# Filter taps carried through DRAM, part of q's feature map on ScalarE, and one transpose for the last 64 features of two chunks

## The chip, the core and the metric

The kernel runs on one core of a Trainium2 chip. The core has a matrix engine (TensorE, in the profile PE, with its weight loads listed apart as PEld), VectorE (DVE), ScalarE (ACT), GpSimd (POOL), and SyncE (SP), which here only issues DMAs. Each engine runs its own instructions in the order in which the program lists them, and waits where data from another engine is missing. The metric is the time of one execution on the device in microseconds (us); smaller is better.

## The reference

The result mixes two branches by a gate, for S = 2048 tokens of D = 448 features:

```python
g = sigmoid((x * gate_w).sum(-1, keepdims=True))
a = A(x, wqkv, wo)          # linear attention, 16 heads of 28 features
b = B(x, ...)               # long convolution along the tokens, plus x * D_skip
return g * a + (1 - g) * b

# A
phi = lambda t: where(t > 0, t + 1, exp(t)) + 1e-6
pq, pk = phi(q), phi(k)
kv = einsum("bhsd,bhse->bhde", pk, v);  z = einsum("bhsd->bhd", pk)
o = einsum("bhqd,bhde->bhqe", pq, kv) / (einsum("bhqd,bhd->bhq", pq, z) + 1e-6)
return o @ wo
```

B convolves every feature with a filter that is built from `log_A_real`, `A_imag`, `C_real`, `C_imag` and `log_dt`.

## The kernel before

The tokens are cut into 16 chunks of 128. Products in near-fp32 precision are made of fp32r pieces: a matrix is split into a rounded high part and the low remainder, and a product takes the high-high, low-high and high-low terms. So one projection of a chunk is 11 matmuls with 128 x 128 weights and about 448 moving columns. The schedule is written by hand: the order of the calls is the order on each engine.

**Start.** `first_d`, the other weights, x and the filter's parameters `abc` (four DMAs of 448 KB, lines 229-230) arrive by DMAs on SP. `load_x` brings in one chunk, `split_t` and `split_n` make its transposed and plain high and low parts (high on ACT, low on POOL).

**Filter.** `s4d_prepare` is a generator that `steps` advances between other work. It computes for each feature whether its filter is a constant over all lags, to the precision needed (`okc`), and the value of that constant (`p0`, 112 partitions x 4). Features that are not constant would need `general_conv`, which is behind a branch at the end and is not entered with these inputs. The generator's last part (lines 311-314) spreads `p0` over 128 partitions: four transposes on PE into the bank "v1", and a copy on ACT into `near`. `do_v(c)` multiplies a chunk by the triangular matrix `tri` (running sums along the tokens, two matmuls), `v_post(c)` multiplies the running sums by `near` on DVE, sends the last row by two small DMAs to `u`, and lets POOL add the product to `y` (`v_add`).

**Main loop** (line 476, c = 2 to 13). An iteration projects k of chunk c+1 (`project`, bank "k"), runs `k_feature`, `k_high`, `k_low` on it, projects q of chunk c (bank "q"), runs `q_post`, and accumulates `do_g(c)`, ten matmuls of pk's parts with x into four banks that stay open over all chunks. `VS` (line 35) lists which `do_v` go into which iteration. `q_post` uses `feature`: exp on ACT, then on DVE a clamp (`t = min(e, 1) + 1e-6`, line 350) and `max(q + 1 + 1e-6, t)` into `pq` (line 353). In iteration 5 come the four transposes (`steps(1)`, line 496), `v_post(0)`, `do_v(1)` and `v_post(1)`.

**Middle.** After chunk 15's k the sums are turned into `kv`, which is multiplied with `wo` to give the rows `mh`, `ml`.

**Attention loop** (line 814, c = 0 to 15). For each chunk `norm_a` (POOL) and `norm_b` (DVE) form the denominators, `norm_d` inverts them for two chunks at a time (DVE, then a copy on ACT, line 556), and `norm_c` divides pq by them into `pn`, a tile of 4 x 128 columns: three column blocks j = 0, 1, 2 of 112 + 16 features, and a block j = 3 that holds the last 64 features twice (POOL, line 573). `turn_pe` transposes the four blocks on PE into the PSUM tile "tr" (line 604), `turn_split` makes the high part `th` on ACT (line 611) and the low part `tl` on DVE (line 612). In block 3 the transposed features stand in partitions 0 to 63 and again in 64 to 127, since one half meets the high and the other the low part of the weights. `tail` (line 615) puts rows for the convolution's part of earlier chunks into the low part. `attend` multiplies with 11 matmuls (line 629), and `final_b` adds y and sends the chunk out. The loop runs `turn(c+1)` ahead of `attend(c)`.

## Time and profile before

| What | Value |
|---|---|
| Time, median of 3 runs | 173.89 us (173.82 to 174.45) |
| The profiled execution's own time | 174.06 us |
| Its span, first to last instruction | 172.2 us |
| Instructions | 2796 |
| Bytes moved by DMA | 18.60 MB, mean 108 GB/s |

The busy time in the stages, as the view by windows gives it:

| Stage | us from the start | PE | DVE | ACT | POOL |
|---|---|---|---|---|---|
| start, first chunks | 5.0 to 46.6 | 41.60 | 30.32 | 30.08 | 26.51 |
| rest of the main loop | 47 to 118 | 71.00 | 40.35 | 35.33 | 55.33 |
| middle | 118 to 127 | 9.00 | 8.06 | 5.81 | 7.69 |
| attention, chunks 0 to 11 | 127 to 158 | 31.00 | 28.28 | 17.49 | 26.42 |
| attention, the rest | 158 to 169 | 11.00 | 5.47 | 4.68 | 1.11 |

A row of the profile's timeline reads: start, length, engine, line of the kernel, operation, tile written <- tiles read, shape, count, and in brackets the idle time before it and what ended it. Matmuls overlap each other, so their pace is read from start to start and not from their length. A group row of the view by lines ends in busy time and the mean length of one in ns, then the idle time before.

### The profile page before, as it was taken

Reading aid. Unit: us, or ns where it says so; the run is one execution under the profiler, and the core shown is the slowest. Engines: PE = TensorE matmul, PEld = TensorE weight load, DVE = VectorE, ACT = ScalarE, POOL = GpSimd, SP = SyncE. Lnnn points to the kernel's source line nnn. Section 1 sums busy time; section 2 is a strip of 40 time slices with the busy share of each in tenths; the row PEclk is TensorE's granted clock in tenths of the full one; section 3 lists DMA queues with packets and bytes.
Section 4 is the critical chain, followed back from the end, with each engine's and each line's share of the span. In section 5 each row is a group of like instructions: output and inputs, shape, how many; then the busy total and the mean of one; then the engine's idle time right before and its main releaser. Section 6 shows DMA issues by size and latency. Waiting matters only on the chain. (4 is left out here: it accounts for less than half of the span.)

```text
span 172.2 us, 2796 instructions
## 1 busy us (share of the span) xinstructions
PE 167.8 (97%) x876; PEld 152.0 (88%) x876; DVE 113.9 (66%) x240; ACT 96.0 (56%) x221; POOL 120.0 (70%) x128
## 2 busy tenths in 40 slices
PE   6999999999999999999999999999999999999992
PEld 2788999999899999999999999999899999999992
DVE  0847737698975483846627346487898998987542
ACT  3688588894256262542727456356574564664541
POOL 6082667877529988696996999529968998892200
PEclk9999999999999999999999999999999999999999
DMA  5989975097003031230404200000031222122213
GB/s 173 415 297 294 268 209 166 0 368 303 4 0 114 11 123 34 95 123 1 122 15 131 106 1 1 0 0 2 7 67 54 107 89 76 62 99 107 108 59 108
DMA packets 7962, 18.60 MB, mean 108 GB/s; under 512 B 2045, under 2 KB 4810, under 8 KB 7818
## 3 DMA queue, kind: packets, MB, share of 16 engines
q1 hardware_dynamic: 7802, 18.30, 32.0%
q8 instruction: 7, 0.11, 0.3%
q10 hardware_dynamic: 144, 0.11, 0.2%
q14 instruction: 9, 0.07, 0.1%
HBM read 14.38 MB, written 3.67 MB: 105 GB/s over the span
## 5 line engine op out<-in xcount | busy, mean ns | idle before, releaser
L629 PE MATMUL a<-wk,th 128*128 128x448 f32 (+1 forms) x170 | 36.4, 360 | 0.0
L403 PE MATMUL g<-pkh,xn 128*128 128x448 f32 x112 | 35.6, 364 | 0.0
L629 PEld LDWEIGHTS a<-wk,th 128*128 128x128 f32 x170 | 29.5, 189 | 1.6
L334 PE MATMUL k<-wk,xt 128*128 128x448 f32 x132 | 29.3, 367 | 0.0
L334 PE MATMUL q<-wqh,xt 128*128 128x450 f32 x120 | 27.5, 366 | 0.0
L362 DVE SCALAR_TENSOR_TENSOR k<-k,e 128x448 f32<-128x448 f32 x12 | 7.6, 632 | 29.4 <-ACT e L361 29.4
L423 POOL TENSOR_TENSOR y<-y,t 128x448 f32<-128x448 f32 x16 | 18.7, 1168 | 11.5 <-DVE t L415 11.5
L334 PEld LDWEIGHTS k<-wk,xt 128*128 128x128 f32 x132 | 24.8, 189 | 2.2 <-DVE wk L236 0.3
L334 PEld LDWEIGHTS q<-wqh,xt 128*128 128x128 f32 x120 | 22.5, 188 | 1.7
L236 POOL TENSOR_TENSOR xn<-xr,xn 128x448 fp32r<-128x448 f32 x16 | 19.4, 1211 | 6.6 <-ACT xn L246 4.5
L403 PE MATMUL g<-pkl,xn 128*128 128x448 f32 x64 | 23.4, 366 | 0.0
L403 PEld LDWEIGHTS g<-pkh,xn 128*128 128x128 f32 x112 | 21.0, 188 | 2.2
L236 POOL TENSOR_TENSOR xt<-xr,xt 128x512 fp32r<-128x512 f32 x14 | 18.2, 1297 | 5.9 <-ACT xt L240 5.9
L360 ACT ACTIVATE e<-k 128x448 f32<-128x448 f32 x12 | 6.5, 544 | 26.9 <-PE k L334 26.9
L542 POOL TENSOR_TENSOR prod<-pq,zb 128x448 f32<-128x448 f32 x16 | 18.6, 1172 | 4.1 <-ACT zb L665 3.0
L252 POOL TENSOR_TENSOR y<-xr,rows 128x448 f32<-128x448 f32 x16 | 18.8, 1175 | 0.0
L567 POOL TENSOR_TENSOR pn<-pq,den 128x336 f32<-128x336 f32 x16 | 12.3, 771 | 5.9 <-ACT den L556 4.1
L634 DVE SCALAR_TENSOR_TENSOR ot<-y,og,a 128x448 f32<-128x448 f32 (+1 forms) x17 | 10.7, 629 | 5.1 <-PE a L629 5.1
L612 DVE TENSOR_TENSOR th<-tr,th 128x512 fp32r<-128x512 f32 x16 | 11.0, 691 | 2.7 <-ACT th L611 2.1
L403 PEld LDWEIGHTS g<-pkl,xn 128*128 128x128 f32 x64 | 11.2, 174 | 1.2 <-DVE pkl L372 0.2
L611 ACT CAST th<-tr 128x512 fp32r<-128x512 f32 x16 | 9.4, 588 | 4.6 <-PE tr L604 4.4
L334 PE MATMUL q<-wql,xt 128*128 128x450 f32 x45 | 11.6, 364 | 0.0
(150 smaller groups left out, 302.3 us busy)
## 6 DMA issues: line engine op xcount, KB each, us to landing
xr<-in SPq DMA_DIRECT2D x15, 512.0 KB, 6.2
out<-ot SPq DMA_DIRECT2D x15, 224.0 KB, 1.9
pq<-in SPq DMA_DIRECT2D x4, 448.0 KB
wvo<-in SPq DMA_DIRECT2D x1, 1792.0 KB
y<-in SPq DMA_DIRECT2D x2, 480.0 KB
y<-in SPq DMA_DIRECT2D x2, 450.0 KB
u<-t SPq DMA_DIRECT2D x30, 1.8 KB, 1.7
y<-in SPq DMA_DIRECT2D x1, 448.0 KB, 4.3
```

What stands on the lines that cost most here:

```text
L236: eng.tensor_tensor(out=o, in0=r, in1=h.bitcast(F32), op=ALU.subtract)
L252: POOL.tensor_tensor(out=y[:, c], in0=plain[c][:, :D], in1=dsk, op=ALU.mult)
L334: PE.matmul(o[:, :n], lhsT=a, rhs=b, start=run.n == 1, stop=not seq)
L362: DVE.scalar_tensor_tensor(out=pks[c], in0=pks[c], scalar=1.0, in1=e, op0=ALU.add, op1=ALU.max)
L403: PE.matmul(g[i][:a.shape[1], :D], lhsT=a, rhs=b, start=c == 0 and n == 0, stop=c == NC - 1 and n == len(seq) - 1)
L423: POOL.tensor_tensor(out=y[:, c], in0=y[:, c], in1=t, op=ALU.add)
L542: POOL.tensor_tensor(out=pd[c], in0=pq[:, c], in1=zb, op=ALU.mult)
L567: POOL.tensor_tensor(out=n[:, :3, :DJ].rearrange("p j (h d) -> p j h d", h=4), in0=a, in1=r[:, :H - 4].rearrange("p (j h) -> p j h", j=3)[ ...
L611: ACT.copy(h, ov)
L612: DVE.tensor_tensor(out=l, in0=ov, in1=h.bitcast(F32), op=ALU.subtract)
L629: PE.matmul(a[:, lo:hi], lhsT=u_, rhs=w_[:, lo:hi], start=n == 0, stop=n == 10)
L634: DVE.scalar_tensor_tensor(out=ot[:, lo:hi], in0=y[:, c, lo:hi], scalar=og[:, c:c + 1], in1=a[:, lo:hi], op0=ALU.mult, op1=ALU.add)
```

## The change

It has four parts.

1. **Taps through DRAM.** The four transposes and the copy of lines 311-314 go. Instead iteration 5 writes `p0` to a DRAM tile `nd` and loads it back, spread over 128 partitions, into the row of `pq` that belongs to chunk 15 and is still free (`taps`). The products of chunks 0 to 3 (`v_post`) read `taps`, in iteration 6; ACT then copies `taps` into `near` for the later chunks. `VS` becomes a pair of lists for each iteration, and POOL's additions are collected in `adds` and issued by `v_adds`. From iteration 5 on x is loaded one iteration earlier.
2. **q's clamp on ScalarE.** For chunks 4 to 13 `q_post` computes exp(-relu(-q)) with two ACT instructions and one DVE instruction, `max(q + 1, e)`; `q_shift` adds 1e-6 on ACT later.
3. **A shared transpose.** `norm_pair(c)`, for even c, fills block 3 of `pn` with the last 64 features of chunk c and of chunk c+1 in place of the same 64 twice. An odd chunk has three transposes. `turn_split` of an even chunk has one more ACT copy (64 partitions, 128 columns), and that of an odd chunk takes block 3 from the even chunk's PSUM tile: two ACT copies and a DVE subtraction of 64 partitions x 128 columns, then the other three blocks as 384 columns.
4. **Filter parameters** `abc` come by two DMAs in place of four.

```diff
-VS = {c: (2 * c - 10, 2 * c - 9) for c in range(5, 11)} | {c: (c + 1,) for c in range(11, NC - 1)}
+VS = {c: ((2 * c - 10,), (2 * c - 9,)) for c in range(5, 11)} | {c: ((c + 1,), ()) for c in range(11, NC - 1)}
+VS[5], VS[6] = ((0,), ()), ((), (2, 3))
...
-    for i in range(4):
-        SP.dma_start(out=abc[:, i], in_=abc_d[:, i])
-        if i == 0:
-            load_x(4)
+    SP.dma_start(out=abc[:, :2], in_=abc_d[:, :2])
+    load_x(4)
+    SP.dma_start(out=abc[:, 2:], in_=abc_d[:, 2:])
...
-        yield
-        o = ps.tile([P, 512], F32, name="p", tag="v1")
-        for j in range(J):
-            PE.transpose(o[:, j * DJ:(j + 1) * DJ], p0[:, j:j + 1].to_broadcast([DJ, P]), ident[:DJ, :DJ])
-        ACT.copy(near, o[:, :D])
...
     def q_post(c, o, mid=None):
         ACT.activation(e1[:, c:c + 1], o[:, D:D + 1], AF.Exp, scale=-1.0)
-        feature(pq[:, c], o, mid)
+        if 3 < c < NC - 2:
+            e = tp.tile([P, D], F32, name="e", tag="e")
+            ACT.activation(e, o[:, :D], AF.Relu, scale=-1.0)
+            ACT.activation(e, e, AF.Exp, scale=-1.0)
+            DVE.scalar_tensor_tensor(out=pq[:, c], in0=o[:, :D], scalar=1.0, in1=e, op0=ALU.add, op1=ALU.max)
+        else:
+            feature(pq[:, c], o, mid)
+
+    def q_shift(c):
+        ACT.add(pq[:, c], pq[:, c], 1e-6)
...
+    taps = pq[:, NC - 1].rearrange("p (r j) -> p j r", j=J)
+
-    def v_post(c):
+    def v_post(c, w=None):
+        w = near.rearrange("p (j r) -> p j r", j=J) if w is None else w
         t = tp.tile([P, D], F32, name="t", tag="v0")
-        DVE.tensor_tensor(out=t, in0=vt.pop(c)[:, :D], in1=near, op=ALU.mult)
+        DVE.tensor_tensor(out=t.rearrange("p (j r) -> p j r", j=J),
+                          in0=vt.pop(c)[:, :D].rearrange("p (j r) -> p j r", j=J), in1=w, op=ALU.mult)
         if c < NC - 1:
             for k in (c, UL + c):
                 SP.dma_start(out=u[k:k + 1], in_=t[P - 1:P])
-            v_add(c, t)
+            adds.append((c, t))
         return t
...
     for c in range(2, NC - 2):
-        if c + 3 < NC:
-            load_x(c + 3)
+        for i in (c + 3,) if c < 5 else (c + 3, c + 4) if c == 5 else (c + 4,):
+            if i < NC:
+                load_x(i)
...
+        if c == 5:
+            SP.dma_start(out=nd.rearrange("o (r j) -> (o r) j", j=J), in_=p0)
+            SP.dma_start(out=pq[:, NC - 1], in_=nd.to_broadcast([P, D]))
...
         split_t(c + 2)
+        if c == 6:
+            v_post(0, taps)
+            v_post(1, taps)
+        v_adds()
         k_feature(c + 1, ko)
...
         qo = project(c, wqh, wql, D + 2, "q")
-        if c == 5:
-            steps(1)
-        else:
-            for v in vs[1:]:
-                do_v(v)
+        for v in vs[1]:
+            do_v(v)
         q_post(c, qo)
...
-        if c == 5:
-            v_post(1)
+        if c > 3:
+            q_shift(c)
+        if c == 6:
+            ACT.copy(near.rearrange("p (j r) -> p j r", j=J), taps)
...
+    def norm_pair(c):
+        b = pq[:, c:c + 2, 3 * DJ:].rearrange("p b (h d) -> p b h d", h=4)
+        POOL.tensor_tensor(out=pn[c][:, 3].rearrange("p (b h d) -> p b h d", b=2, h=4), in0=b[:, :, :, DS:],
+                           in1=dn[c // 2][:, :2, H - 4:, None].to_broadcast([P, 2, 4, DH - DS]), op=ALU.mult)
...
     def turn_pe(c):
...
-        for j in range(J):
+        for j in range(J - c % 2):
             PE.transpose(o[:, j * P:(j + 1) * P], n[:, j], ident)
...
+    halves = []
+
     def turn_split(c, o):
+        low = lambda l, a, h: DVE.tensor_tensor(out=l, in0=a, in1=h.bitcast(F32), op=ALU.subtract)
+        ov = o.rearrange("p (j t) -> p j t", j=J)
         t = xt_p.tile([P, 2, J, P], F32R, name="th", tag="t")
         h, l = th[c], tl[c] = t[:, 0], t[:, 1]
-        ov = o.rearrange("p (j t) -> p j t", j=J)
-        ACT.copy(h, ov)
-        DVE.tensor_tensor(out=l, in0=ov, in1=h.bitcast(F32), op=ALU.subtract)
+        if c % 2:
+            b = halves.pop()
+            for p in (slice(DT, P), slice(DT)):
+                ACT.copy(h[p, 3], b)
+            low(l[:DT, 3], b, h[DT:, 3])
+            ACT.copy(h[:, :3], ov[:, :3])
+            low(l[:, :3], ov[:, :3], h[:, :3])
+        else:
+            halves.append(ov[DT:, 3])
+            ACT.copy(h, ov)
+            ACT.copy(h[DT:, 3], ov[:DT, 3])
+            low(l, ov, h)
...
     kv_high(1, k1)
+    norm_pair(0)
     norm_c(1)
```

`norm_c` calls `norm_pair(c)` for the other even chunks, and block 3 of the odd chunks is no longer written. The additions by `v_adds` stand after the k-projection's `split_t`, after `k_high`, and after `q_post`, but in iteration 6 not after `q_post`.

More of the change, by code (lines that the diff above doesn't have):

```diff
@@ L186, in gated_mix_kernel @@
     ps = work.enter_context(tc.tile_pool(name="ps", bufs=1, space=PSUM))
+    nd = work.enter_context(tc.tile_pool(name="nd", bufs=1, space=bass.MemoryType.DRAM)).tile([1, D], F32, name="nd")
     warm = tp.tile([P, 512], mybir.dt.bfloat16, name="warm", tag="e")
@@ L282, in s4d_prepare @@
         junk = [yf[:DJ, F0 + (i - 2) * 2 * N:F0 + (i - 1) * 2 * N].rearrange("p (i n) -> p i n", i=2) for i in range(2)]
-        s0, s1, dt, am, p0, p1, d2, md, b0, b1 = (small() for _ in range(10))
+        s0, s1, dt, am, p1, d2, md, b0, b1 = (small() for _ in range(9))
         for j in range(J):
@@ L418, in v_post, with v_adds @@
                 SP.dma_start(out=u[k:k + 1], in_=t[P - 1:P])
-            v_add(c, t)
+            adds.append((c, t))
         return t
+    adds = []
+    def v_adds():
+        while adds:
+            v_add(*adds.pop(0))
     def v_add(c, t):
         POOL.tensor_tensor(out=y[:, c], in0=y[:, c], in1=t, op=ALU.add)
+    p0 = small()
     prep = s4d_prepare()
@@ L490, in gated_mix_kernel @@
         if c > 5:
-            for v in vs[:1]:
+            for v in vs[0]:
                 v_post(v)
+        v_adds()
         k_low(c + 1)
         qo = project(c, wqh, wql, D + 2, "q")
-        if c == 5:
-            steps(1)
-        else:
-            for v in vs[1:]:
-                do_v(v)
+        for v in vs[1]:
+            do_v(v)
         q_post(c, qo)
@@ L502, in gated_mix_kernel @@
             split_n(c + 2)
-        if c == 5:
-            v_post(0)
-        else:
-            for v in vs[1:]:
-                v_post(v)
+        for v in vs[1]:
+            v_post(v, taps if c == 6 else None)
+        if c != 6:
+            v_adds()
         if c < 5:
@@ L524, in gated_mix_kernel @@
             split_n(c + 2)
-        if c == 5:
-            v_post(1)
+        if c > 3:
+            q_shift(c)
+        if c == 6:
+            ACT.copy(near.rearrange("p (j r) -> p j r", j=J), taps)
         for j in {11: (0, 1), 12: (2, 3)}.get(c, ()):
@@ L572, in norm_c @@
                           in1=dp[0][:, c, H - 4:, None, None].to_broadcast([P, 4, 3, DS // 3]), op=ALU.mult)
-        POOL.tensor_tensor(out=n[:, 3].rearrange("p (b h d) -> p b h d", b=2, h=4),
-                          in0=b[:, None, :, DS:].to_broadcast([P, 2, 4, DH - DS]),
-                          in1=r[:, None, H - 4:, None].to_broadcast([P, 2, 4, DH - DS]), op=ALU.mult)
+        if c and c % 2 == 0:
+            norm_pair(c)
     def phi(c):
```

4 lines of the change are left out of this document (2 added, 2 removed).

## The prediction

> **What bounds the kernel now.** I read the head of the page first, then the list of waits, then the timeline.
>
> ```profile
> span 172.2 us, 2796 instructions
> PE 167.8 (97%) x876; PEld 152.0 (88%) x876; DVE 113.9 (66%) x240; ACT 96.0 (56%) x221; POOL 120.0 (70%) x128
> PEclk9999999999999999999999999999999999999999
> GB/s 173 415 297 294 268 209 166 0 368 303 4 0 114 11 123 34 95 123 1 122 15 131 106 1 1 0 0 2 7 67 54 107 89 76 62 99 107 108 59 108
> ```
>
> PE is busy 97% of the span at the full granted clock. A busy PE need not be at its pace, so the waits matter: in the list of waits for PE alone there is one row, at the very start.
>
> ```profile
> PE q L258 <- POOL warm L189: 1.3, 1, 1.3
> ```
>
> So from the first real matmul to the last, PE issues without a recorded wait. Such a kernel gets shorter only by what PE no longer issues, and longer only where another engine falls behind PE. Both have to be priced. The pace comes from the timeline, start to start:
>
> ```profile
> 46.66 0.60 PE L313 MATMUL p<-both,sm 112*128 112x112 f32 x4
> ...
> 47.31 0.36 PE L403 MATMUL g<-pkl,xn 128*128 128x448 f32 x1
> ...
> 57.17 2.36 PE L334 MATMUL k<-wk,xt 128*128 128x448 f32 x11
> 59.37 0.36 PE L410 MATMUL v<-xn,tri 128*128 128x448 f32 x1
> ...
> 134.48 0.60 PE L604 MATMUL tr<-both,pn 128*128 128x128 f32 x4
> ...
> 137.14 0.60 PE L604 MATMUL tr<-both,pn 128*128 128x128 f32 x4
> 137.50 2.26 PE L629 MATMUL a<-wk,th 128*128 128x448 f32 x10
> ...
> 153.10 0.27 PE L589 MATMUL o<-both,og 128*1 128x128 f32 x1
> 153.22 0.60 PE L604 MATMUL tr<-both,pn 128*128 128x128 f32 x4
> ```
>
> Eleven matmuls take 59.37 - 57.17 = 2.20, 0.20 each. A chunk of the attention loop takes 137.14 - 134.48 = 2.66 for 11 matmuls and 4 transposes, so the four cost 2.66 - 2.20 = 0.46, 0.115 each.
>
> **What the change takes off PE.** The four transposes of `p0`: from 46.66 to the second g matmul at 47.31 are 0.65 for these four and one matmul of 0.20, so 0.45 goes. The odd chunks lose one transpose of four: 8 x 0.115 = 0.92. Whether the fourth costs a quarter of the four can be doubted; the row at 153.10 is a transpose alone, 0.12 before the next start, so the price is per piece. Sum: -1.37.
>
> The Trainium skill, "TensorE: Matmul & The Clock Gate", section Back-to-back issue gap, gives about 81 ns for a pair of weight load and matmul at 128 columns. By that estimate the 12 transposes are worth 0.97, and the sum would be 0.40 worse; the rows above show 0.11 to 0.12, and I go by them.
>
> **What it adds, first in the attention loop.** Here PE waits for the weights `th` (ACT), then `tl` (DVE). These are the rows of the turns of chunks 2 to 5, and the load of `attend(4)`:
>
> ```profile
> 130.43 0.69 DVE L612 TENSOR_TENSOR th<-tr,th 128x512 fp32r<-128x512 f32 x1 [0.26 <-ACT th L611]
> ...
> 133.85 0.69 DVE L612 TENSOR_TENSOR th<-tr,th 128x512 fp32r<-128x512 f32 x1
> ...
> 135.34 0.37 DVE L553 RECIPROCAL den<-den 128x32 f32<-128x32 f32 x1
> ...
> 136.44 0.69 DVE L612 TENSOR_TENSOR th<-tr,th 128x512 fp32r<-128x512 f32 x1
> ...
> 138.45 0.69 DVE L612 TENSOR_TENSOR th<-tr,th 128x512 fp32r<-128x512 f32 x1
> ```
> ```profile
> 135.73 0.19 ACT L556 COPY den<-den 128x32 f32<-128x32 f32 x1 [0.87 <-DVE den L553]
> 135.82 0.59 ACT L611 CAST th<-tr 128x512 fp32r<-128x512 f32 x1
> 136.31 0.54 ACT L640 COPY pq<-a 128x448 f32<-128x448 f32 x1
> ```
> ```profile
> 137.47 0.91 PEld L629 LDWEIGHTS a<-wk,th 128*128 128x128 f32 x5
> ```
>
> An even chunk's turn is the tight one, since the denominators go before it on the same engines: DVE's reciprocal ends at 135.71, ACT's copy of it starts at 135.73, `th` ends at 136.41, `tl` starts at 136.44 and ends at 137.13. `attend(4)` needs `tl` with its second weight load, about 0.18 after 137.47, at 137.65: 0.52 to spare. Odd chunks have no such chain and are ready earlier: `tl` of chunk 5 is done at 139.14.
>
> The new pieces have no row of their own; these are the nearest:
>
> ```profile
> L745 ACT CAST kvh<-tr 112x224 fp32r<-112x224 f32 x1 | 0.3, 346 | 0.8 <-DVE tr L734 0.8
> L748 DVE TENSOR_TENSOR kvl<-k,kvh 112x224 fp32r<-112x224 f32 x1 | 0.4, 392 | 0.4 <-ACT kvh L745 0.4
> ```
>
> From 224 columns (0.346) to 512 (0.59) ACT adds 0.85 ns a column, so a copy of 128 takes about 0.265. After `th` ACT's next instruction starts 0.49 on, though `th` is 0.59 long (135.82, 136.31): the extra copy ends 0.49 + 0.265 - 0.59 = 0.17 later than `th` alone. Without that overlap it would be 0.30. On DVE, 224 columns take 0.392 and 512 take 0.69: 0.29 for 128, 0.56 for 384. With the overlap of about 0.09 between DVE's instructions an odd turn occupies it for 0.20 + 0.47 in place of 0.60, 0.07 more; at the worst, if 128 columns cost what 224 do, 0.17 more.
>
> I leave out the 0.45 that shifts everything alike. `tl(2)` at 130.43 waited for ACT: PE's transposes come 0.115 earlier, the extra copy is 0.17 long, so it starts 0.06 later (up to 0.19). From there DVE works without a pause up to 136.44, so delays add: 0.06 (chunk 2) + 0.07 (chunk 3) + 0.17 (chunk 4) = 0.30, at the worst 0.19 + 0.17 + 0.30 = 0.66. `tl(4)` is then done at 137.43. PE has meanwhile lost three transposes (chunks 1, 3, 5) and wants it at 137.65 - 0.35 = 137.30. It waits 0.13, and 0.05 for the signal: about **+0.2**, at the least nothing, at the worst 0.55. I take 0.2, since ACT's rows here do overlap.
>
> It isn't paid for each chunk. `tl(3)` to `tl(5)` is 138.45 - 133.85 = 4.60 on the chain, and 4.84 with 0.07 + 0.17; PE's two chunks take 5.32 - 0.115 = 5.20. So the chain gains over 0.3 a pair. Chunk 8 is the other tight place, behind the late part of chunk 15's q:
>
> ```profile
> 144.54 1.23 POOL L542 TENSOR_TENSOR prod<-pq,zb 128x448 f32<-128x448 f32 x1
> ...
> 144.97 1.05 DVE L799 TENSOR_SCALAR t<-e 128x448 f32<-128x448 f32 x1
> ...
> 147.33 0.69 DVE L612 TENSOR_TENSOR th<-tr,th 128x512 fp32r<-128x512 f32 x1
> ...
> 148.14 2.06 PE L629 MATMUL a<-wk,th 128*128 128x448 f32 x9
> ```
> ```profile
> L350 DVE TENSOR_SCALAR t<-e 128x448 f32<-128x448 f32 x15 | 10.0, 665 | 1.9 <-ACT e L349 1.9
> ```
>
> `tl(8)` is done at 148.02, wanted at about 148.3: 0.3 to spare, against 0.17 + 0.07 + 0.115 = 0.36 by the change. But line 799 took 1.05 here, to just behind POOL's product (145.77), and the same form at line 350 takes 0.665 in the mean. POOL loses block 3 of chunks 5, 7 and 9 by then, 0.4 each, so its product is over earlier, and I expect those 0.4 back on DVE. Nothing here; at the worst 0.17 + 0.30 + 0.115 - 0.3 = 0.3.
>
> POOL alone gains in this loop, eight pieces less. Block 3 of chunk 0 now waits for chunk 1's denominators, as chunk 1's `pn` does:
>
> ```profile
> 121.34 0.76 POOL L567 TENSOR_TENSOR pn<-pq,den 128x336 f32<-128x336 f32 x1
> ...
> 123.00 0.60 PE L604 MATMUL tr<-both,pn 128*128 128x128 f32 x4
> ```
>
> The pair goes ahead of that row, where it delays nothing, since POOL has lost chunk 0's block before; it is done over a microsecond before PE's transposes at 123.00.
>
> **What it adds in the main loop.** The way of the taps, with the rows that price it:
>
> ```profile
> 46.44 0.16 DVE L280 TENSOR_TENSOR sm<-sm,okc 112x4 f32<-112x4 f32 x1
> ...
> 53.39 0.63 DVE L362 SCALAR_TENSOR_TENSOR k<-k,e 128x448 f32<-128x448 f32 x1 [2.32 <-ACT e L361]
> ...
> 55.18 0.61 DVE L372 SCALAR_TENSOR_TENSOR zb<-k,zb 128x448 f32<-128x448 f32 x1
> ```
> ```profile
> u<-t SPq DMA_DIRECT2D x30, 1.8 KB, 1.7
> ...
> cst<-in SPq DMA_DIRECT2D x1, 112.5 KB, 3.8
> ...
> ldt<-in SPq DMA_DIRECT2D x1, 1.8 KB, 10.1
> ```
>
> `p0` is ready at 46.60. The write (1.8 KB) is nearest to u<-t, 1.7; the spread load (224 KB) to cst, 3.8: landed at about 52.1. Before DVE starts k of chunk 7 at 53.39 - 0.45 = 52.94 it has two products of about 0.55 to do, so from 51.8 on it starts late. PE notices only when bank "k" isn't free: its last reader ends at 55.79, PE writes it at 57.17, 1.38 to spare. PE stands still from a landing at 51.8 + 1.4 = 53.2 on. I take nothing, with 1.1 in hand.
>
> Queued behind the two waiting DMAs on SP are chunk 10's x (wanted two iterations, about 14 us, later) and the rows of `u`, wanted at the end of the loop; behind the products on DVE is k's feature, priced above; behind the collected additions on POOL are `split_t`'s and `split_n`'s low parts. For these, and for ACT's two more instructions, the cover is idle time in each iteration:
>
> ```profile
> 52.20 0.54 ACT L360 ACTIVATE e<-k 128x448 f32<-128x448 f32 x1 [2.46 <-PE k L334]
> ```
> ```profile
> 65.36 1.15 POOL L423 TENSOR_TENSOR y<-y,t 128x448 f32<-128x448 f32 x1 [1.59 <-DVE t L415]
> ```
>
> ACT gets 0.54 + 0.55 (a relu and `q_shift`) and has 2.46 free; `q_shift` waits for DVE, and behind it stands a `split_t` that PE wants a whole iteration later. POOL has four additions in iteration 7 where it had two, 2.3 more, and gets 1.59 back in each of the next two. Without the cover k's feature would be late, and PE after 1.38. DVE loses line 350 in ten chunks, which nobody waits for. The merged loads of `abc` cost nothing: the slice row shows no traffic in the eighth slice (30 to 34 us), so the queue is empty well before the main loop needs it.
>
> **The sum.** -0.45 - 0.92 + 0.2 = -1.17. The profiled execution took 174.06, so 172.9; it lies 0.17 over the median of the runs, and against the median of 173.89 I predict **172.7**, -0.7%. Less than 0.5% (0.87) is what a measurement of this kernel can hardly tell from no change. The forecast's own range is 172.4 (no wait, and a fourth transpose that costs a weight load more) to 173.0.
>
> **The rivals.**
> - *ACT and DVE in the even turns give more of it back.* At the worst 0.55 at chunk 4 and 0.3 at chunk 8: -1.37 + 0.85 = -0.52, 173.4. For it: DVE is without pause there. Against: the chain gains on PE after each pair.
> - *The odd chunks gain little*, because PE's time there is a fixed price of changing over to transposes: -0.45 + 0.2 and some of the 0.92, 173.0 to 173.6. The lone transpose at 0.12 speaks against. The 81 ns of the Trainium skill's page would give 173.1.
> - *The taps come late: slower.* The write to DRAM is in 112 pieces. ldt, of the same size, took 10.1 amid the first loads; then the taps land at 46.6 + 10.1 + 3.8 = 60.5, PE waits 60.5 - 53.2 = 7.3, and the time is 180.0. It gets slower than before from a landing at 53.2 + 1.2 = 54.4, by over 0.5% from 55.3. Against it: the slice row has 4 GB/s in the eleventh slice (43 to 47 us), so nothing is ahead in the queue. The Trainium skill, "DMA: Bandwidth & Descriptors", section Anatomy of one DMA, puts about 2 us on each small transfer and warns of a long receipt when the target is HBM; two of these make 4, an estimate that would land at 50.6.
>
> **Chances.** Forecast 0.58; the turns 0.20; the odd chunks 0.13; late taps 0.07; faster than 172.4 0.02. The range of 172.3 to 173.6 leaves out the late taps and about a tenth besides. Faster by over 0.5% means under 173.0: the forecast, what is faster still and a small part of the odd chunks' case, 0.62. Within 0.5%: the rest of the two rivals above, and a tap little late, 0.32. Slower: late taps, 0.06.
>
> **What would show it.** No matmul at line 313; 56 transposes in place of 64; odd chunks 2.55 apart from even ones' 2.66; if the wait is there, PEld idle on the low parts near chunk 4's `attend`, 0.1 to 0.3; `taps` landed before DVE is done with chunk 5; no PE wait at bank "k" in iteration 7. I am wrong if PE waits repeat in every even chunk (the chain is longer than worked out), if the pace of odd chunks stays at 2.66, or if PE stands still between 50 and 60 us.

## The result

The changed kernel takes 175.01 us in the median of 14 runs (174.56 to 176.6) against 173.96 us for the kernel before (14 runs, 173.75 to 174.6): a ratio of 1.0063, 95% interval 1.0050 to 1.0076. It is 1.05 us slower. The forecast was 172.7, in a range of 172.3 to 173.6.

The profiled execution took 175.15 us, 1.09 more than that of the kernel before. The head of the page after:

```profile
span 173.2 us, 2789 instructions
PE 167.6 (97%) x864; PEld 150.2 (87%) x864; DVE 111.0 (64%) x238; ACT 113.9 (66%) x265; POOL 116.9 (67%) x120
PEclk9999999999999999999999999999999999999999
```

PE has 12 matmuls less at the same clock, as the forecast said, and VectorE and GpSimd are less busy too. Only ScalarE has more to do, 17.9 us. No busy share says why it is slower. The waits do. For PE, and for PE's weight loads (of these the rows behind the start):

```profile
...
PE k L330 <- ACT wk L449: 0.4, 1, 0.4
PE tr L631 <- DVE th L637: 0.2, 1, 0.2
```
```profile
PEld a L669 <- DVE th L637: 0.9, 3, 0.4
PEld tr L631 <- issue: 0.8, 2, 0.5
...
PEld v L415 <- DVE t L423: 0.3, 1, 0.3
...
PEld k L330 <- ACT e L380: 0.2, 1, 0.2
```

The row of `wk` lies in the beginning, where both kernels load their first weights. New are the others: a PE wait in front of transposes, and loads that wait for the low parts of the attention (`a`), in front of the transposes (`tr`), for the bank of a product (`v`) and for bank "k" (the list names ScalarE's `e` for this one; it is traced to VectorE further down).

Three rows in each timeline cut the execution into stages that don't depend on how the beginning went: the first product of `v`, the first transposes of the attention loop, the last matmul.

```profile
44.01 0.36 PE L410 MATMUL v<-xn,tri 128*128 128x448 f32 x1
...
168.83 0.27 PE L629 MATMUL a<-rc,th 112*128 112x224 f32 x1
```
```profile
44.04 0.36 PE L415 MATMUL v<-xn,tri 128*128 128x448 f32 x1
...
122.97 0.60 PE L631 MATMUL tr<-both,pn 128*128 128x128 f32 x4
...
169.38 0.27 PE L669 MATMUL a<-rc,th 112*128 112x224 f32 x1
```

(The first fence is before, the second after; before, the first transposes stand at 123.00.)

| Stage | before | after | difference | forecast |
|---|---|---|---|---|
| main loop: first v to first transposes | 123.00 - 44.01 = 78.99 | 122.97 - 44.04 = 78.93 | -0.06 | -0.45 |
| attention: first transposes to last matmul | 168.83 - 123.00 = 45.83 | 169.38 - 122.97 = 46.41 | +0.58 | -0.92 + 0.2 |
| close: last matmul to the end of the span | 172.2 - 168.83 = 3.37 | 173.2 - 169.38 = 3.82 | +0.45 | 0 |

With 0.03 ahead of the first `v` and 0.09 outside the span (1.95 against 1.86) that makes the 1.09. The page prints the span to a tenth of a us, so a close is good to 0.05, here and below. All three stages came out worse than forecast. These are the rows of chunk 4's turn after, which answer to those shown of before (VectorE, then ScalarE, then the loads of `attend(4)`):

```profile
134.14 0.88 DVE L637 TENSOR_TENSOR th<-tr,th 64x128 fp32r<-64x128 f32 x2
134.94 0.62 DVE L570 TENSOR_REDUCE den<-prod 128x16 f32<-128x448 f32 x1
...
137.22 0.69 DVE L637 TENSOR_TENSOR th<-tr,th 128x512 fp32r<-128x512 f32 x1 [0.41 <-ACT th L651]
```
```profile
136.30 0.59 ACT L650 CAST th<-tr 128x512 fp32r<-128x512 f32 x1
136.93 0.26 ACT L651 CAST th<-tr 64x128 fp32r<-64x128 f32 x1
137.21 0.53 ACT L680 COPY pq<-a 128x448 f32<-128x448 f32 x1
```
```profile
134.55 0.42 PEld L631 LDWEIGHTS tr<-both,pn 128*128 128x128 f32 x4 [0.51 <-issue]
...
137.96 0.70 PEld L669 LDWEIGHTS a<-wk,th 128*128 128x128 f32 x4 [0.29 <-DVE th L637]
```

The extra copy (line 651) begins when the copy ahead of it is done (136.30 + 0.59 = 136.89, then 136.93); VectorE's low part starts only behind it, at 137.22 in place of 136.44, and PE's load waits 0.29. The odd turn ahead holds VectorE from 134.14 to 134.94, 0.80 where it was 0.60. And chunk 4's transposes wait 0.51: their bank was chunk 2's, and chunk 3's turn still reads chunk 2's other half from it at 134.14.

The pace shows that this comes again. The transposes of chunks 3 to 10 start at:

```profile
131.72 0.49 PE L631 MATMUL tr<-both,pn 128*128 128x128 f32 x3
134.58 0.63 PE L631 MATMUL tr<-both,pn 128*128 128x128 f32 x4 [0.16 <-DVE th L637]
137.26 0.49 PE L631 MATMUL tr<-both,pn 128*128 128x128 f32 x3
140.09 0.60 PE L631 MATMUL tr<-both,pn 128*128 128x128 f32 x4
142.74 0.49 PE L631 MATMUL tr<-both,pn 128*128 128x128 f32 x3
145.29 0.60 PE L631 MATMUL tr<-both,pn 128*128 128x128 f32 x4
147.94 0.49 PE L631 MATMUL tr<-both,pn 128*128 128x128 f32 x3
151.01 0.63 PE L631 MATMUL tr<-both,pn 128*128 128x128 f32 x4
```

Chunk 7 has the forecast's 2.55 (145.29 - 142.74). Chunk 3 takes 2.86, chunk 5 2.83 and chunk 9 3.07, all of them longer than the 2.66 of before.

### The profile page after: what moved, and what is told of

It is laid out like the page before. It is cut to its first block, busy times and chain, and to the rows that moved or that the text cites. A ratio compares the mean times of both kernels' runs of the same rounds, so it can differ in the third digit from the quotient of the medians.

```text
span 173.2 us, 2789 instructions
## 1 busy us (share of the span) xinstructions
PE 167.6 (97%) x864; PEld 150.2 (87%) x864; DVE 111.0 (64%) x238; ACT 113.9 (66%) x265; POOL 116.9 (67%) x120
## 5 line engine op out<-in xcount | busy, mean ns | idle before, releaser
L669 PE MATMUL a<-wk,th 128*128 128x448 f32 (+1 forms) x170 | 37.2, 362 | 0.1
L637 DVE TENSOR_TENSOR th<-tr,th 128x512 fp32r<-128x512 f32 (+2 forms) x24 | 12.3, 514 | 4.4 <-ACT th L651 2.6
L362 ACT ACTIVATE pkh<-k 128x448 fp32r<-128x448 f32 x12 | 6.5, 546 | 10.0 <-DVE k L358 10.0
```

Of the source, the lines that this page charges most:

```text
L637: low = lambda l, a, h: DVE.tensor_tensor(out=l, in0=a, in1=h.bitcast(F32), op=ALU.subtract)
L669: PE.matmul(a[:, lo:hi], lhsT=u_, rhs=w_[:, lo:hi], start=n == 0, stop=n == 10)
```

## The experiments

Theory A is what these rows say: the attention loop's 0.58 comes from the shared transpose alone, the rest from the taps and the close. The rivals are in the expectations. All stages below are read from the same three rows of each kernel's timeline, the blocks (how many pieces of the program the instruction queue loaded) from that queue's row of its page.

| Run | time, us (runs) | ratio to before, 95% interval | main loop | attention | close | blocks |
|---|---|---|---|---|---|---|
| e1 shared transpose alone | 174.53 (12) | 1.0037 [1.0022, 1.0051] | 78.96 | 46.40 | 3.38 | 9 |
| e2 all but that | 174.64 (12) | 1.0040 [1.0021, 1.0058] | 78.89 | 45.78 | 3.90 | 10 |
| e3 clamp alone | 174.31 (12) | 1.0015 [0.9998, 1.0032] | 79.26 | 45.84 | 3.65 | 9 |
| e4 taps alone | 174.81 (12) | 1.0049 [1.0028, 1.0071] | 81.02 | 45.84 | 3.88 | 10 |
| e5 e1, duplicate late | 173.72 (12) | 0.9979 [0.9967, 0.9992] | 78.98 | 45.47 | 3.37 | 9 |
| e6 e1, third bank | 174.40 (12) | 1.0032 [1.0017, 1.0046] | 78.99 | 46.41 | 3.41 | 9 |
| e7 e1, split in the even chunk | 175.00 (6) | 1.0048 [1.0031, 1.0065] | 78.98 | 46.54 | 3.40 | 9 |
| e8 changed, four transposes at the end | 174.99 (6) | 1.0058 [1.0038, 1.0077] | 79.06 | 46.40 | 3.89 | 10 |
| e9 changed, duplicate late | 174.08 (12) | 1.0007 [0.9991, 1.0023] | 79.10 | 45.44 | 3.82 | 10 |
| e10 e5, third bank, blocks first | 173.56 (12) | 0.9968 [0.9954, 0.9982] | 79.02 | 45.34 | 3.43 | 9 |
| e11 no taps | 173.41 (7) | 0.9964 [0.9949, 0.9980] | 78.50 | 45.84 | 3.42 | 9 |
| e12 p0 also to DRAM | 175.04 (1) | | 79.00 | 45.84 | 4.41 | 10 |
| e13 e2, late but straight | 173.99 (1) | | 78.71 | 45.83 | 3.95 | 10 |
| e14 e2, strided but early | 174.35 (1) | | 78.72 | 45.83 | 3.60 | 9 |
| e15 p0 also to SBUF | 175.00 (1) | | 78.97 | 45.81 | 4.41 | 10 |

The kernel before took 173.95 to 173.98 in the median beside each of these groups. What lies ahead of the first `v` differs from one execution to the next (43.7 to 44.5 us), so single times say less than the stages. Six executions have the old main loop unchanged (before, e1, e5, e6, e7 and e10) and lie within 0.06 there, 78.96 to 79.02; those with the old turns lie within 0.06 in the attention. e12 to e15 are single executions. e2's median is 0.69 over the kernel before, while its stages make less than 0.4; its profiled execution, 174.13, is one of the shortest of its twelve, and the rest is left open.

**Which part does it: e1 to e4.** e1 is the kernel before with `norm_pair`, the three transposes and the new `turn_split`; e2 is the changed kernel with the old ones:

```diff
+    norm_pair(0)
     norm_c(1)
...
-        for j in range(J):
+        for j in range(J - c % 2):
```

> The kernel before, with the shared transpose of the last 64 features alone. Theory A (the loss is made in the attention loop): the trace of the changed kernel gains eight transposes of about 0.11 us there, some 0.9, and loses about 1.45 in PE waits in front of the transposes of chunks 4 and 10 and in the attends of chunks 4, 8, 10 and 12; so here the last matmul starts 0.5 to 0.7 us later than in the kernel before, counted from the first transpose, and the time is 0.5 to 1.1 us longer (the upper end if the close of the program grows by 0.45 too). Rival B (the turns gain by themselves what was forecast, and lose only because the main loop hands over its work at other times): 0.5 to 0.9 us shorter. Rival C (the attention loop breaks even and the loss is the close of the program): the last matmul within 0.15 of the kernel before.

> The changed kernel with its old transposes: the taps through DRAM and q's clamp on ScalarE alone. Theory A: the main loop gains 0.45 and gives 0.40 back (0.16 at bank k of chunk 7, 0.24 at the banks of chunks 2 and 3), so the time is within 0.2 us of the kernel before, or 0.45 above it if the close of the program grows with this part. Rival B: as slow as the changed kernel, plus 1.0. Rival D (the main loop's gain is real and lost later in the turns): 0.3 to 0.5 shorter.

e1's attention is 46.40 and e2's 45.78: the whole 0.58 comes from the shared transpose, whatever the main loop does. Rivals B and C fall, and rival D too, since e2 isn't shorter. e2's main loop keeps 0.10 of the 0.45; its close has the 0.45 more.

e3 puts part 2 into the kernel before, e4 parts 1 and 4:

> The kernel before, with q's clamp and shift on ScalarE alone. Theory A: no change, within 0.15 us; no new PE wait in the main loop. Rival: ScalarE's two more instructions an iteration make the feature of k late, 0.1 or more in single iterations, and PE waits at bank k in several of them: 0.3 us longer or more.

> The kernel before, with the taps through DRAM alone (q's clamp stays on VectorE, which has 0.38 us more to do in each of ten iterations). Theory A: within 0.2 us of the kernel before; PE waits for the banks of chunks 2 and 3 as in the changed kernel (0.24 in all, since the two strided products are the cause). Rival (the clamp on ScalarE is what pays for the late taps): VectorE is later by 0.38 at those products and PE waits 0.5 or more there, 0.2 to 0.4 longer than the kernel before.

e3's interval reaches 1, but its main loop is 0.27 longer: theory A was wrong that the clamp costs nothing (below). e4 settles nothing on its question. Its profiled execution lost 1.7 us ahead of the taps, where VectorE fell behind and PE waited for `pq` (this row), and its median can't be told from e2's.

```profile
46.06 0.65 PE L330 MATMUL q<-wqh,xt 128*128 128x450 f32 x2 [1.74 <-DVE pq L349]
```

**What in the shared transpose: e5, e6, e7.** e5 moves one copy:

```diff
             ACT.copy(h, ov)
-            ACT.copy(h[DT:, 3], ov[:DT, 3])
+            dups[c] = (h[DT:, 3], ov[:DT, 3])
             low(l, ov, h)
...
     def tail(c):
+        if c in dups:
+            ACT.copy(*dups.pop(c))
```

> The shared transpose alone (as in e1), but in the even chunks ScalarE's copy of the 64 duplicated rows is issued behind its copy of the finished chunk, so that VectorE's low part no longer waits for it. Theory A1 (the duplicate in front of the low part, 0.33 us in every even chunk, is what PE waits for in the attends of chunks 4, 8, 10, 12 and 14): the idle time of VectorE behind that copy goes, some 0.7 of the 1.45 us of waits goes with it, and from the first transpose to the last matmul it takes 45.6 to 45.8 instead of 46.40 (45.83 before). Theory A2 (the PSUM buffer held into the odd chunk) alone: 46.1 to 46.4, with the waits in front of the transposes of chunks 4 and 10 unchanged. Theory A3 (VectorE's and ScalarE's work for a pair is longer than PE's 5.2 us, so that every saving counts): 45.3 to 45.7 and those waits smaller too.

45.47: the loop is 0.93 shorter than in e1 and 0.36 shorter than before, and the kernel is faster than before by 0.21%. This is more than theory A1's 0.7 and lies in theory A3's range. But A3's signs are missing: the waits in front of the transposes haven't shrunk (0.6 and 0.3 us, in e1 0.5 and 0.3), and in the changed kernel the chain from one even low part to the next takes 5.03 (137.22 to 142.25), less than PE's 5.2. The rows of the same turn in e5:

```profile
137.05 0.69 DVE L614 TENSOR_TENSOR th<-tr,th 128x512 fp32r<-128x512 f32 x1
```
```profile
136.43 0.59 ACT L627 CAST th<-tr 128x512 fp32r<-128x512 f32 x1
136.92 0.54 ACT L661 COPY pq<-a 128x448 f32<-128x448 f32 x1
137.78 0.26 ACT L635 CAST th<-tr 64x128 fp32r<-64x128 f32 x1 [0.32 <-DVE th L614]
```

The low part starts at 137.05, right behind `th` (136.43 + 0.59 = 137.02), and the duplicate is made at 137.78, long before PE wants it with the tenth of eleven matmuls. In e5's list of waits no `a` is left; only `tr` is:

```profile
PEld tr L608 <- POOL pn L564: 0.6, 1, 0.6
PEld tr L608 <- issue: 0.3, 1, 0.3
```

The first of them names GpSimd's `pn`, but that was done at 134.01 and the load begins at 134.67; the transpose itself names VectorE's `th`, the reader of the bank.

e6 gives the transposes a third bank, taken from the attention products:

```diff
+        pool, tag = ((p3, "tr"), (p3, "tr"), (ps, "k"))[c % 3]
-        o = p3.tile([P, 512], F32, name="tr", tag="tr")
+        o = pool.tile([P, 512], F32, name="tr", tag=tag)
...
-            pool, tag = ((p3, "a"), (p3, "a"), (ps, "v0"), (ps, "k"))[(c + i) % 4]
+            pool, tag = ((p3, "a"), (p3, "a"), (ps, "v0"))[(c + i) % 3]
```

> The shared transpose alone (as in e1), with three PSUM banks for the transposes and three instead of four for the attention products. Theory A2 (the even chunk's bank is held until VectorE has taken the low part of the odd chunk's 64 features from it, and the next even chunk's transposes wait): the waits in front of the transposes of chunks 4 and 10, 0.3 each, go, and from the first transpose to the last matmul it takes 45.8 instead of 46.40. Theory A3 (VectorE is late there in any case): PE waits a few matmuls later, in the attends of chunks 3 and 9, for the low part itself, and it stays at 46.2 to 46.4.

46.41, nothing gained, as theory A3 said. Of the 0.51 in front of chunk 4's transposes 0.17 is left, now for VectorE's part of `pn` (done at 133.92, the load at 134.03), and PE stands a few matmuls later for the low part (chunk 3, then chunk 4):

```profile
134.88 1.71 PEld L647 LDWEIGHTS a<-wk,th 128*128 128x128 f32 x9 [0.28 <-DVE th L615]
...
137.78 1.31 PEld L647 LDWEIGHTS a<-wk,th 128*128 128x128 f32 x7 [0.36 <-DVE th L615]
```

So the wait named "tr" was not the bank's doing alone: VectorE was late by as much.

e7 takes VectorE's extra instruction away altogether. The even chunk's one pass gives the low part of both halves, and ScalarE carries the rest over in `tail`:

```diff
+            for p in (slice(DT, P), slice(DT)):
+                ACT.copy(t[p, 0, 3], ov[DT:, 3])
+            ACT.copy(th[c][DT:, 3], ov[:DT, 3])
+            ACT.copy(t[:DT, 1, 3], tl[c][DT:, 3].bitcast(F32))
```

> The shared transpose alone, with the odd chunk's 64 features split in the even chunk: VectorE's one pass over the even chunk's four blocks takes the low part of both halves, ScalarE copies the odd chunk's two high halves, the duplicate and the odd chunk's low half late in the even chunk, and the odd chunk has three blocks left for both engines (VectorE 0.27 and a wait less in odd chunks, the bank free in the even chunk, ScalarE one copy more in a pair). Theory A1 with A2: 44.95 to 45.2 from the first transpose to the last matmul, the 0.88 of the eight transposes gained, and a time 0.6 to 0.9 us under the kernel before. Theory A3: the same. Rival (PE's time there isn't set by these chains, and fewer transposes bring nothing): 45.8 or more. Rival (ScalarE's five copies late in the even chunk become the wait): PE waits for th or for the tail rows in the even chunks, 45.3 to 46.

A miss: 46.54. It is in the numbers of the first rival, but e5 had already shown that PE's time does follow these chains. What the trace shows is the second rival, with a larger price. The copies stand ahead of its copy of the denominators, and VectorE, which has less to do, now waits 0.64 for that, where it waited 0.32 in the changed kernel:

```profile
132.97 0.30 ACT L638 CAST th<-th 64x128 fp32r<-64x128 f32 x1
133.30 0.30 ACT L639 CAST th<-rows 48x128 fp32r<-48x128 f32 x1
133.62 0.19 ACT L556 COPY den<-den 128x32 f32<-128x32 f32 x1
```
```profile
133.91 0.63 DVE L547 TENSOR_REDUCE den<-prod 128x16 f32<-128x448 f32 x1 [0.64 <-ACT den L556]
```

Of its 1.05 us over the kernel before, 0.71 is in the attention; 0.37 lies ahead of the first `v`, where its code is the same as before. That is left open.

**The mended versions: e9, e10.** e9 is the changed kernel with e5's edit. e10 is e5 with e6's banks, and with the three blocks of the odd chunk split ahead of the 64 features:

```diff
             b = halves.pop()
+            ACT.copy(h[:, :3], ov[:, :3])
+            low(l[:, :3], ov[:, :3], h[:, :3])
             for p in (slice(DT, P), slice(DT)):
                 ACT.copy(h[p, 3], b)
             low(l[:DT, 3], b, h[DT:, 3])
-            ACT.copy(h[:, :3], ov[:, :3])
-            low(l[:, :3], ov[:, :3], h[:, :3])
```

> The whole changed kernel with the duplicate copied late, as in e5. Theory: the stages add up. Main loop from the first product of v to the first transpose 78.9 (as in the changed kernel), from there to the last matmul 45.47 (as in e5), the close 3.8 to 3.9 (as in every kernel with the taps through DRAM); 0.9 us under the changed kernel, 174.1, within 0.3 of the kernel before. Rival (the saving in the attention loop needs the main loop of the kernel before): 46 or more in the loop and 174.6 or more.

> The shared transpose alone, with the duplicate copied late, the third transpose bank, and in the odd chunk the three whole blocks split ahead of the 64 features. Theory A3 (chain and bank together; either alone is paid for by the other): the wait in front of chunk 4's transposes, 0.4 in e5, goes and doesn't come back in chunk 3's attend; from the first transpose to the last matmul 44.95 to 45.25, the time 0.6 to 0.85 us under the kernel before. Rival (the wait moves on to VectorE's low part, as in e6): 45.45 or more, and the time as e5's, 0.2 under the kernel before.

The stages add up in e9: 174.08, level with the kernel before, 0.9 under the changed kernel. e10 is the fastest kernel here that computes the whole, 0.32% under before, but its 45.34 is 0.13 better than e5 and not 0.4. With a bank free, chunk 4's transposes still wait 0.27, for VectorE's part of `pn` (done at 134.53, the load at 134.64), and two loads behind them wait 0.2 and 0.3: most of the wait moved on again, as the rival said.

**What the taps give back: e11, e13, e14.** e11 takes lines 311 to 314 out of the kernel before; e13 and e14 start from e2. In e11 and e14 the products take the skip weights, so the taps are left out of the result; in e13 they take the taps in a wrong order:

```diff
 e11
-        DVE.tensor_tensor(out=t, in0=vt.pop(c)[:, :D], in1=near, op=ALU.mult)
+        DVE.tensor_tensor(out=t, in0=vt.pop(c)[:, :D], in1=dsk, op=ALU.mult)
 e13
-    taps = pq[:, NC - 1].rearrange("p (r j) -> p j r", j=J)
+    taps = pq[:, NC - 1].rearrange("p (j r) -> p j r", j=J)
 e14
-    taps = pq[:, NC - 1].rearrange("p (r j) -> p j r", j=J)
+    taps = dsk.rearrange("p (r j) -> p j r", j=J)
...
-            SP.dma_start(out=nd.rearrange("o (r j) -> (o r) j", j=J), in_=p0)
-            SP.dma_start(out=pq[:, NC - 1], in_=nd.to_broadcast([P, D]))
```

> The kernel before without the four transposes of p0 and ScalarE's copy behind them; the products take the skip weights instead of the taps, so the taps are left out of the result. It shows what the transposes of p0 cost at most. Theory (bank k is late next): of the 0.45 us about 0.15 is lost again at the first matmul of k of chunk 7, and from the first product of v to the first transpose of the attention it takes 78.65 to 78.75 instead of 78.99; what the changed kernel has above that (78.93) is the price of the late and strided products. Rival (the transposes are hidden anyway): 78.9 to 79.0. Rival (all of it is gained): 78.5 to 78.6. The close shows what a shorter PE program does to it: 3.4 or 3.8.

> The kernel of e2 (old transposes, taps through DRAM, clamp on ScalarE), but the taps are read in the order in which they lie, without the stride, so the products take them in a wrong order; the way through DRAM and the wait for it stay. Theory (the stride costs: two products of 0.95 in place of 0.61 hold the banks of chunks 0 and 1 for 0.3 and 0.7 longer): the 0.24 us of waits in front of the products of chunks 2 and 3 goes and the first transpose of the attention is 78.65 to 78.7 behind the first product of v, in place of 78.89. Rival (the landing costs, the stride doesn't): 78.85 to 78.95. In both the 0.15 at bank k of chunk 7 stays, since it is ahead of the products. The close, 3.8 to 4.4, has the DRAM buffer.

> The kernel of e2 without the way through DRAM: the four first products take the skip weights with the same stride and need no transfer, so the taps are left out of the result. Theory (the stride): 78.8 to 78.9 from the first product of v to the first transpose. Rival (the landing): VectorE does the two products before 52 us and PE waits nowhere for them, 78.65. The close without a DRAM buffer: 3.4 to 3.65 if the buffer is its cause, 3.8 if it lies in the rest of the changed program.

e11: 78.50, so the transposes are worth 0.49 and all of it is gained; the theory that bank "k" would take 0.15 back was wrong for this kernel. e13 and e14: 78.71 and 78.72. Either the stride or the landing can go, and 0.17 to 0.18 of e2's 78.89 comes back; it takes both to make PE wait. (e13's taps land as late as e2's: the products begin 8.48 and 8.46 behind the first `v`.) With both, the price follows the landing. e8 and e9 have the main loop of the changed kernel and of e2, but their products begin 8.63 and 8.64 behind the first `v`, 8.48 in the changed kernel; PE's load waits 0.5 in place of 0.3, and the loop takes 79.06 and 79.10. Over these four executions nothing of the 0.45 is kept. The same two products in e2 and in e13:

```profile
52.29 1.83 DVE L423 TENSOR_TENSOR t<-v,pq 128x448 f32<-128x448 f32 x2 [2.72 <-DMA pq<-nd]
...
54.17 0.19 PEld L415 LDWEIGHTS v<-xn,tri 128*128 128x128 f32 x1 [0.28 <-DVE t L423]
```
```profile
52.19 1.16 DVE L423 TENSOR_TENSOR t<-v,pq 128x448 f32<-128x448 f32 x2 [2.74 <-DMA pq<-nd]
```

The other 0.2 is in e2, e13 and e14 alike, and not in e11: it is the wait at bank "k" of chunk 7, and those three have the clamp. The row of that wait in e11, which has none, and in the changed kernel:

```profile
49.38 2.37 PE L329 MATMUL k<-wk,xt 128*128 128x448 f32 x11
51.59 0.36 PE L405 MATMUL v<-xn,tri 128*128 128x448 f32 x1
```
```profile
49.07 0.37 PE L416 MATMUL v<-xn,tri 128*128 128x448 f32 x1
...
49.33 2.46 PE L330 MATMUL k<-wk,xt 128*128 128x448 f32 x11
51.63 1.80 PE L330 MATMUL q<-wqh,xt 128*128 128x450 f32 x8
```

Eleven matmuls take 2.21 in e11 and 2.30 here, and the first of them starts 0.06 late. The bank's last reader is VectorE's `zb`. ScalarE's `e`, which the list names, comes from bank "q"; the load begins 0.11 to 0.12 behind the end of `zb` in all seven kernels without the transposes of `p0` (e4 apart), e11 among them. `zb` starts 4.34 to 4.39 us behind the first `v` in all nine kernels that leave the clamp on VectorE (e4 apart), and 4.53 to 4.58 in all seven that have it on ScalarE. So the clamp delays it by about 0.19. In e3 the four transposes, which wait for `p0` from the same engine, show the same delay.

**The close: e8, e12, e15.**

```diff
 e8
+    o = p3.tile([P, 512], F32, name="tr", tag="tr")
+    for j in range(J):
+        PE.transpose(o[:, j * P:(j + 1) * P], ident, ident)
     final_b(NC - 1)
 e12
+        SP.dma_start(out=nd.rearrange("o (r j) -> (o r) j", j=J), in_=p0)
 e15
+        SP.dma_start(out=small(), in_=p0)
```

> The changed kernel with four transposes of the identity behind the last matmul, into a free bank that nobody reads, so that PE's program is as long again as in the kernel before. In the kernels with the taps through DRAM the instruction queue loads ten blocks in place of nine, and the end of the span lies 3.8 to 3.9 us behind the last matmul's start, in place of 3.4 to 3.65. Theory (PE's shorter program moves its last branch over the edge of a block): nine blocks again, 3.4 to 3.5 from the last matmul of the attention to the end, and the time 0.4 us under the changed kernel, 174.6. Rival (another engine's program, or the DRAM buffer itself): 3.8 to 3.9 and 175.0 as the changed kernel.

> The kernel before with p0 also written to a DRAM buffer that nobody reads, one DMA of 1.8 KB more and nothing else. Theory (the DRAM buffer is what lengthens the close): 3.8 to 3.9 from the last matmul to the end of the span and ten instruction blocks. Rival (it is where the programs of the changed kernel end): 3.4 and nine blocks.

> The kernel before with p0 also copied by one DMA to a spare place in SBUF that nobody reads: as e12, with SBUF for DRAM. Theory (the DRAM buffer lengthens the close, 4.41 in e12): 3.4 and nine instruction blocks. Rival (one DMA instruction more in SyncE's program does it): 4.4 and ten blocks.

PE's program is not it (e8, with four matmuls more: 3.89; e11, with as many as e2: 3.42). e12 looked like proof that the DRAM buffer is (4.41), until e15 gave the same 4.41 without one. One DMA instruction more on SyncE, in the middle of the program, is enough (single executions both). The row of the instruction queue, before and e15:

```profile
q14 instruction: 9, 0.07, 0.1%
```
```profile
q14 instruction: 10, 0.08, 0.1%
```

All nine kernels with nine blocks, the kernel before among them, close in 3.37 to 3.65, and all eight with ten, the changed kernel among them, in 3.82 to 4.41. Whose time it is can be read from the closing instructions of each engine. These are the DRAINs of SyncE and ScalarE at the end, with their first and last start, before and after:

```profile
L933 SPq DRAIN  x3: 7/13/19, 171.4 to 172.0; - x3
L933 ACTq DRAIN  x2: 8/8/8, 171.3 to 171.9; - x2
```
```profile
L974 SPq DRAIN  x3: 7/7/120, 172.3 to 172.7; - x3
L974 ACTq DRAIN  x2: 8/8/8, 171.8 to 172.7; - x2
```

ScalarE, the last engine with work, comes to its first DRAIN 2.44 to 2.46 us behind the last matmul in all seventeen kernels. SyncE comes to its own 0.04 behind its last wait in all nine with nine blocks, and 0.39 behind it in all eight with ten, where the DRAIN also lasts 0.12 in place of 0.01; from its end to the end of the span it is 0.8 in all. So the growth is SyncE's. In e12 and e15 SyncE also begins its closing waits 2.51 behind the last matmul instead of 0.47, which makes their other 0.5. That the 0.39 is the loading of the tenth block is argued, from its coming with ten blocks only, and why a program gets ten is open: the changed kernel has no more DMAs on SyncE than the kernel before. Open, too, is why e3 and e14 close 0.2 later with nine.

## Why the prediction was wrong

- **"-0.45" for p0's transposes** was right as a price (e11: 0.49).
- **"I take nothing, with 1.1 in hand"** for the taps failed. The landing itself was near the forecast (52.1; the products start at 52.5). But the step looked only at bank "k" of the next iteration. The products also hold the banks `v0` and `v1`, which `do_v(2)` and `do_v(3)` write in the same iteration, and they were priced at 0.55 each where two strided ones take 1.83 to 1.85. That is 0.18 in e2's execution (e13, e14), and up to 0.4 where the taps land later (e8, e9).
- **The cover for "ACT's two more instructions"** was named as ScalarE's idle time. What stands behind ScalarE is `split_n`, behind that GpSimd, and behind that VectorE: 0.19 on `zb`, 0.15 to 0.2 for PE. The step followed the queue one engine far. e3 shows that the clamp does it; that the way leads over GpSimd is read from the rows in the last section. With the price of the taps this leaves the main loop 0.06 and 0.10 in two executions (the changed kernel and e2) and nothing in two others (e8 and e9).
- **"-0.92" for the odd chunks** was right as a price: in e5, the odd chunks without a wait are 2.55 apart, the even ones 2.65 to 2.68.
- **"+0.2", one wait, "isn't paid for each chunk"** is the step that failed most. The 0.92 and a total of 0.58 more mean 1.5 of waits in place of 0.2. The extra copy was taken to overlap with the one ahead of it, 0.17; it takes 0.33 (136.89 to 137.22). An odd turn adds 0.20 to VectorE, not 0.07 (134.14 to 134.94 against 0.60): its two subtractions follow each other without an overlap (0.88 for both). Each is 0.03 over the upper end in the text (0.30 and 0.17). So `tl(4)` is done at 137.91, 0.78 later than before, where 0.30 was forecast and 0.66 was the worst, and PE loses 0.31 in front of chunk 4's transposes and 0.28 in its `attend` (chunk 3's and chunk 5's period against 2.55). Nor does the chain gain "over 0.3 a pair": the prediction's own sum becomes 4.60 + 0.33 + 0.20 = 5.13, the trace has 5.03, and PE's 5.20 leaves 0.07 to 0.17. The `attend` of chunk 6 has no wait, but at chunk 8, the other tight place, for which the text says "nothing here", PE loses 0.52 (chunk 9's period), and at chunks 10 and 12 another 0.17 and 0.10. These are 1.4 of the 1.5. The prediction's own signs for being wrong are in the trace: waits in the even chunks (4, 8, 10 and 12), and PE standing still between 50 and 60 us (0.33 at 54.42). e5 proves the place: with the copy out of the chain 0.93 of the 1.5 goes.
- **The PSUM bank of the even chunk**, held into the odd one's turn, was not in the prediction at all. Taking it away alone gains nothing (e6); with the chain mended 0.4 is left there, in front of chunk 4's transposes, and a third bank, with the odd chunk's blocks split first, gets 0.13 of it (e10).
- **The close** was not in the sum: +0.45, the second largest term, in SyncE's last instructions.
- Of the rivals, the first (the turns give more back) named the right place with 0.85 as its worst. The second, little gained from the odd chunks, was wrong: they gain what was forecast and lose it in waits. The third, late taps, was wrong in its price of 7.3, though the taps do make PE wait. Slower than before had a chance of 0.06, for late taps; it came about in another way.

## What to carry to other kernels

Where two engines feed a bound third one and have hardly any time to spare, a small extra instruction is priced by its place in their chain and not by its length: the same copy cost 0.93 us ahead of the low part, and no wait is seen for it behind. Add up each engine's whole cycle, waits included, and compare it with the bound engine's new and shorter cycle: here 4.60 against 5.32 us for two chunks had become 5.03 against 5.20, and an engine that was once late had hardly anything to catch up with. When a stage's waits are read one by one, take them away together before trusting any: a wait for a bank and a wait for data can be the same lateness under two names.

## What the runs showed of the hardware

- Two ScalarE copies in a row, on all 128 partitions and into different tiles, overlap by 0.10 (135.82 + 0.59 against 136.31, before). The duplicate, which goes to partitions 64 to 127, overlaps with neither neighbour: not with the one ahead, a part of whose tile it overwrites (136.30 + 0.59 = 136.89, then 136.93), and not with the one behind, which writes another tile (136.93 + 0.26 = 137.19, then 137.21). So the overwriting isn't needed for it. In e5, where the next copy goes to the upper partitions as well, the two overlap by 0.10 (137.78 + 0.26 = 138.04, then 137.94). What decides it is not shown; no run sends the duplicate to another tile. The Trainium skill, "ScalarE: Activation LUTs", section What ACT_TABLE_LOAD costs, says that ACTIVATE instructions back to back overlap by about 93 ns; the first pair agrees with it, the duplicate doesn't.
- A VectorE product of 128 x 448 takes 1.16 for two with its second operand in order and 1.83 with a stride of four elements (e13 and e2).
- VectorE's instructions on 112 x 4 elements take about 0.16 each; beside GpSimd they end when GpSimd does. After, in the two engines' rows:

```profile
44.75 1.33 DVE L282 SCALAR_TENSOR_TENSOR sm<-sm 112x4 f32<-112x4 f32 x2
46.00 0.15 DVE L304 TENSOR_SCALAR sm<-sm 112x4 f32<-112x4 f32 x1
```
```profile
44.77 1.29 POOL L237 TENSOR_TENSOR xt<-xr,xt 128x512 fp32r<-128x512 f32 x1
```

  44.77 + 1.29 = 46.06, and VectorE's pair ends at 46.08. The Trainium skill, "SBUF — State Buffer", section SBUF: two separate sides, says that the two engines share a pair of ports, which an instruction of GpSimd, or one of VectorE with two inputs in SBUF, holds as an exclusive lock to its end; this agrees. By these rows it is how the clamp reaches `zb`: ScalarE's later copy makes GpSimd later (42.54 in place of 41.90 for the same instruction), and VectorE's small instructions move with GpSimd's. No run moves GpSimd alone.
- The end of the program costs 3.37 to 4.41 us from the last matmul, depending on code that has nothing to do with it (e12, e15). The difference is SyncE's: in the eight kernels that load ten blocks it stands 0.39 in front of its first closing DRAIN, in the nine others 0.04.
